# FNet mixing and a GELU block: column 128 of the second stage's operand gets products of its own

## The chip, the cores and the metric

The kernel runs on one core of a Trainium2 chip. The metric is the device time of one execution in microseconds (us). It was taken five times for the kernel before, and the median is compared. One execution more was recorded by the hardware profiler; all readings of the profile are from that one.

## The reference

Two blocks follow each other. The first takes, for each of 8 sequences of 3008 positions with 256 features, the real part of a Fourier transform over both axes. The second is a feed-forward block with weights of 256 x 2048 and 2048 x 256 and the quick form of GELU between them.

```python
X = np.fft.fft(x, axis=1)
X = np.fft.fft(X, axis=2)
out = X.real                      # (8, 3008, 256) float32
x2 = out.reshape(8 * 3008, 256)
h = x2 @ w_in                     # (24064, 2048)
g = h * (1.0 / (1.0 + np.exp(-1.702 * h)))
y = g @ w_out                     # (24064, 256)
```

## The kernel before

The transform over 3008 = 47 x 64 positions is done in two stages. The features are folded first: since the input is real, columns 0 to 128 of the folded operand carry the even part (the sums of feature d and feature 256 - d), columns 129 to 255 the odd part. The transform over the features itself is folded into the weights `wcs` of the feed-forward block.

The first stage (`mix1`, and `mix_first` for sequence 0) takes the products over the 47 positions of a residue class. Its results are written to DRAM (`spill`) and read back in another layout (`fill`) as the tile `t4`: 128 partitions, 12 groups (`NG`) and 256 columns. The partitions of `t4` are two halves of 64 rows (`u` = 0 and 1); in each half 32 rows hold the cosine and 32 the sine parts.

The second stage (`stage2(b, blk)`, line 337) makes from four groups of `t4` the two planes `pq[:, 0]` and `pq[:, 1]` of one block of sequence `b`. Three blocks (`NBLK`) make a sequence, and 24 blocks the run. Its weights are `m2` (`m2f` for sequence 0): 128 partitions, two sets of 64 columns, the cosine set (index 0) and the sine set (index 1), each used in two runs of 32 columns (`h`). Its 32 products run in four nested loops: `cs` over the two planes, `h` over the two runs, `g` over four slices of 32 columns, `u` over the two halves of the rows. Each product has 64 rows, 32 columns of weights and a moving operand of 4 groups by 32 columns; so it uses a 64 x 32 part of the array, and the eight products of one `cs` and `h` use eight different parts. The plane `cs` = 0 takes columns 0 to 127 of `t4` with the cosine weights, the plane `cs` = 1 takes columns 128 to 255 with the sine weights. Four transposes on VectorE (line 354) bring the result into `pq`.

Column 128 (the first one of the plane `cs` = 1) belongs to the even part, yet meets the sine weights there. So `rotate` (line 330) prepares it: one product over all 128 rows with the table `rot`, which exchanges the cosine and the sine rows with a sign, into a PSUM bank `psr`, and a copy back over column 128 of `t4`. It is called nine times: for groups 0 to 3 of sequence 0 just ahead of `stage2(0, 0)` with the copy on ScalarE, for groups 4 to 11 of sequence 0 at step 4, and once for each of the sequences 1 to 7, at step 36 of the sequence ahead (39 for the first), with the copies on VectorE. The stage for that sequence's block 0 is called at step 40.

The order of the work is written out by hand. The main loop has 384 steps, 48 for a sequence (3 blocks, 2 halves, 8 pairs of feed-forward columns). Each step issues the products of the feed-forward block (`halves`, line 495, and `small_products`, line 659), the activations and the sums, and at its end whatever `at(t, ...)` has registered for it: loads, folds, `mix1`, `rotate`, `spill`, `fill` and `stage2`. The engines run their queues in this order and wait for each other by semaphores.

The PSUM banks of the opening (before step 8) are handed out in a round robin of six (`spare`, line 164): each call of `bank` without a tag takes the bank that was handed out longest ago. `rotate` takes one for `psr` like everything else. At step 5 the list is made anew from the banks `o2`, `o3`, `o4` in their order at that time and `b2`; the products `pa` and `pb` of `hidden(5)` go to `b0` and `b1` by name. From step 8 on, `rotate` takes `b2`.

The table `small`, with `m2f`, `m2`, `rot` and the weights `cd` of the features, is loaded by one DMA on SyncE's queue between the first two parts of `w_in` (line 842).

Of the kernel before, what the change touches and what calls it, by code (L numbers as in the profile page):

```python
# [27 lines left out]
F32 = mybir.dt.float32  # L28
# [6 lines left out]
NA, NB = 47, 64  # L35
NJ = NB // 2
# [3 lines left out]
NU, NG = 2, 12  # L40
RUN = 32
# [9 lines left out]
def free(ap, offset, *dims):  # L51
    return bass.AP(ap.tensor, ap.offset + offset, [list(ap.ap[0])] + [list(d) for d in dims])


def kp(u, a):

    n, i = a // 4, 2 * (a % 4) + u
    return 8 * n + i if n else 7 - i


def tables(S, D):

    assert S == NA * NB and D == 256
    H = D // 2
    ks = np.array([kp(u, a) for a in range(NG) for u in range(NU)])
    s = NB * np.arange(NA)[:, None, None] + np.arange(NB)[None, :, None]
    angle = 2.0 * np.pi * ((s * ks) % S) / S
    cos, sin = np.cos(angle), np.sin(angle)
    w1 = np.zeros((NA, NJ + 3, NG * NU, 2))
    w1[:, 1:NJ, :, 0], w1[:, 1:NJ, :, 1] = cos[:, 1:NJ], sin[:, 1:NJ]  # L70
    e0, o0, e1, o1 = ENDS
    w1[:, e0, :, 0], w1[:, o0, :, 0], w1[:, e1, :, 1], w1[:, o1, :, 1] = cos[:, 0], sin[:, 0], cos[:, NJ], sin[:, NJ]


    w0 = np.zeros((128, NJ + 1, NG * NU, 2))
    low, high = w0[0:2 * NA:2], w0[1:2 * NA:2]
    low[:] = w1[:, :NJ + 1]
    high[:, 1:NJ, :, 0], high[:, 1:NJ, :, 1] = cos[:, NJ + 1:], -sin[:, NJ + 1:]
    high[:, e0, :, 1], high[:, o0, :, 1] = cos[:, NJ], sin[:, NJ]
    odd = np.arange(128)[:, None] % 2  # L80
    kinds = np.concatenate([1.0 - odd, odd, -1.0 * odd, 1.0 - 2.0 * odd], 1)

    c, q = np.divmod(np.arange(NJ), 16)
    m2 = []
    for jj in np.where(c, 16 + q, np.where(q, 16 - q, 0)), 4 * (q // 2) + 2 * (q % 2) + c:
        j, k2 = jj[:, None], np.arange(NB)[None, :]
        beta = 2.0 * np.pi * ((j * k2) % NB) / NB
        m = np.zeros((NU, 2, NJ, 2, NB))
        m[:, 0, :, 0], m[:, 1, :, 0] = np.cos(beta), -np.sin(beta)
        m[:, 0, :, 1], m[:, 1, :, 1] = np.sin(beta), np.cos(beta)  # L90
        m[:, :, 0, 0] = m[:, :, 0, 1] = np.stack([np.ones(NB), 1.0 - 2.0 * (np.arange(NB) % 2)])
        m2.append(m)
    rot = np.zeros((NU, 2, NJ, NU, 2, NJ))
    for i in range(NU):
        for n in range(NJ):
            rot[i, 0, n, i, 1, n], rot[i, 1, n, i, 0, n] = (1.0, -1.0) if n else (0.0, 0.0)
        rot[i, 0, 0, i, 0, 0] = rot[i, 1, 0, i, 1, 0] = 1.0

    m, d = np.arange(D)[:, None], np.arange(H)[None, :]
    phi = 2.0 * np.pi * ((m * d) % D) / D  # L100
    cd = np.stack([np.cos(phi), -np.sin(phi)], 1)
    cd[:, 1, 0] = 1.0 - 2.0 * (np.arange(D) % 2)
    cd = cd.reshape(2, H, 2, H).transpose(1, 0, 2, 3)
    small = [t.reshape(128, -1) for t in (*m2, rot, cd)]
    pad = 64 - NM
    w1 = np.pad(w1.reshape(NA, -1), ((0, 128 - NA), (0, pad)))
    w0 = np.concatenate([w0.reshape(128, -1), np.zeros((128, pad)), kinds], 1)
    return np.concatenate([w0, w1], 1).astype(np.float32), np.concatenate(small, 1).astype(np.float32)
# [3 lines left out]
def kernel(ctx: ExitStack, tc, x, w_in, w_out, tab1, tab2, out):  # L112
    nc = tc.nc
    B, S, D = x.shape
    DF = w_in.shape[1]
    H = D // 2
# [4 lines left out]
    const = ctx.enter_context(tc.tile_pool(name="const", bufs=1, space=SB))  # L121
# [10 lines left out]
    Td = [nc.dram_tensor(f"Td{b}", (NG * 128, D), F32, kind="Internal").ap() for b in range(B)]  # L132

    w1 = const.tile([128, (NJ + 3) * NM + 64 - NM], F32, tag="w1", name="w1")
    small = const.tile([128, 4 * NB + 128 + 4 * H], F32, tag="small", name="small")
    m2f, m2 = (small[:, i * 2 * NB:(i + 1) * 2 * NB].rearrange("p (c n) -> p c n", c=2) for i in range(2))
    rot = small[:, 4 * NB:4 * NB + 128]
    cd = small[:, 4 * NB + 128:].rearrange("p (i c d) -> p i c d", i=2, c=2)
    wcs = [const.tile([128, DF], F32, tag=f"wcs{i}", name=f"wcs{i}") for i in range(2)]

    wot = const.tile([128, 2, NF // 2, 4, H], F32, tag="wo", name="wo")
# [24 lines left out]
    def bank(name, tag=None):  # L166
        if tag is None:
            tag = spare.pop(0)
            spare.append(tag)
        if tag in ("o0", "o1"):  # L170
            return o_banks[int(tag[1])]
        return (rest if tag[0] == "o" else psp).tile([128, 512], F32, tag=tag, name=name)
# [5 lines left out]
    t4t, pqt, nbt = {}, {}, {}  # L178
# [148 lines left out]
            t4t[b] = tp.tile([128, NG, D], F32, tag="t4", name="t4")  # L327
        nc.sync.dma_start(out=t4t[b][:, a0:a1, :], in_=Td[b].rearrange("(a p) d -> p a d", p=128)[:, a0:a1, :])

    def rotate(b, a0=0, a1=NG, copy=None):  # L330

        col = t4t[b][:, a0:a1, H]
        ps = bank("psr")
        nc.tensor.matmul(ps[:, 0:a1 - a0], lhsT=rot, rhs=col, start=True, stop=True)
        (copy or nc.vector.tensor_copy)(col, ps[:, 0:a1 - a0])

    def stage2(b, blk):

        pq, t4 = pqp.tile([128, 2, 512], F32, tag="pq", name="pq"), t4t[b]
        pqt[b, blk] = pq  # L340
        m = m2 if b else m2f
        ps = [bank("ps2") for _ in range(NU)]
        for cs in range(2):
            for h in range(2):
                for g in range(4):
                    for u in range(NU):
                        rows, at = slice(64 * u, 64 * u + 64), cs * 256 + h * 128
                        nc.tensor.matmul(ps[u][32 * g:32 * g + 32, at:at + 128], lhsT=m[rows, cs, h * RUN:(h + 1) * RUN],  # L348
                                         rhs=t4[rows, 4 * blk:4 * blk + 4, cs * H + 32 * g:cs * H + 32 * g + 32],
                                         start=(cs == h == 0), stop=True, skip_group_check=True)  # L350
        for u in range(NU):
            for cs in range(2):

                nc.vector.transpose(free(pq[:], cs * 512 + u * RUN, [256, 2], [NU * RUN, 4], [1, RUN]),
                                    free(ps[u][:], cs * 256, [128, 2], [32, 4], [1, 32]))
# [32 lines left out]
    def squares(key, eng):  # L388
        g, hi = pre[key][0], raw[key][:, :, 1].bitcast(F32)
        if eng is nc.scalar:  # L390
            eng.activation(g[:], hi, ACTF.Square)
        else:
            eng.tensor_tensor(g[:], hi, hi, op=ALU.mult)

    def clamp(key, lo=0, n=1024):
        nc.gpsimd.tensor_scalar(pre[key][1][:, lo:lo + n], raw[key][:, lo:lo + n, 1].bitcast(F32), scalar1=TOP, scalar2=-TOP,
                                op0=ALU.min, op1=ALU.max)
# [490 lines left out]
    prepare(out0)  # L888
    finish_in(1)
    clamp(out0)  # L890
    rotate(0, 0, 4, nc.scalar.copy)
    squares(out0, nc.scalar)
    stage2(0, 0)
    warm(1)
    low_up(out0)
# [11 lines left out]
    def at(t, fn, *args):  # L907
        extra.setdefault(t, []).append((fn, args))

    n = len(steps)  # L910
# [11 lines left out]
    if B > 1:  # L922
        at(3, turn, 1)
        at(3, load_x, 1)
    at(4, rotate, 0, 4, NG)
    for i in range(NCK):
        at(7 + i, differences, i)
        at(8 + i, small_weights, i)
    for b in range(B):
        t0 = b * NBLK * NF  # L930
        late = 0 if b else 5
        if b + 2 < B:
            at(t0 + 10, turn, b + 2)
        if b + 1 < B:
            for c in range(NCH):
                for part in range(2):
                    at(t0 + 6 + 2 * c + part + late, fold1, b + 1, c, part, nc.gpsimd)
                if c % 2:
                    at(t0 + 9 + 2 * c + late, mix1, b + 1, c // 2)
            at(t0 + 24 + late, spill, b + 1)  # L940
            at(t0 + 29 + late, fill, b + 1)
            if b + 2 < B:
                at(t0 + 33 + late, load_x, b + 2)
            at(t0 + 36 + 3 * (late > 0), rotate, b + 1)
        for blk in range(NBLK):
            nxt = (b, blk + 1) if blk + 1 < NBLK else (b + 1, 0)
            if nxt[0] < B:
                at(t0 + blk * NF + 8, stage2, *nxt)
                at(t0 + blk * NF + 9, nyquist, *nxt)

    for t in range(n + LAG):
        if t < NP:
# [20 lines left out]
            if t == NP - 1:  # L973
                doubled(NP)
                middle(NP + 1)
        else:
            after, special = (any(fn in (mix1, stage2) for fn, _ in extra.get(k, ())) for k in (t - 1, t))
            if t < n:
                begin(t, 1)
# [78 lines left out]
```

## Time and profile before

| | |
|---|---|
| median of five runs | 1876.68 us |
| lowest and highest of them | 1874.21 and 1879.91 us |
| the profiled execution, its time | 1878.87 us |
| its span, from the first to the last instruction | 1876.8 us |
| mean granted TensorE clock | 0.998 |
| products of the second stage, L348 (records) | 1536 |
| transposes behind them, L354 | 96, mean 416 ns, 28.6 us of waiting for L348 in all |
| corrections, L334 (records) | 18 |
| their copies, L335 | 8 on VectorE, median 173 ns; 1 on ScalarE, 165 ns |

By stretches of the span, the busy time of the engines in us is:

| stretch | length | PE | DVE | ACT | POOL | DMA share |
|---|---|---|---|---|---|---|
| 0 to 37 | 37.0 | 32.0 | 26.9 | 21.7 | 17.0 | 0.85 |
| 37 to 60 | 23.0 | 22.2 | 20.2 | 19.3 | 13.1 | 0.99 |
| 60 to 90 | 30.0 | 29.6 | 19.4 | 18.0 | 14.7 | 0.71 |
| 90 to 125 | 35.0 | 32.0 | 31.2 | 15.7 | 27.6 | 0.47 |
| 125 to 350 | 225.0 | 221.3 | 185.0 | 135.8 | 121.5 | 0.32 |
| 350 to 1876.8 | 1526.8 | 1516.8 | 1249.0 | 938.7 | 770.2 | 0.31 |

PE is TensorE's matmuls, PEld its loads of weights, DVE VectorE, ACT ScalarE, POOL GpSimd, SP SyncE. A product in float32 leaves two loads and two matmul records (two passes), so a count of records is twice the count of products. [...] the pace is read from the distance of the starts. A line number in the profile is that of the kernel before.

### The profile page before, as it was taken

How to read it: one execution, taken by the hardware profiler on the slowest of the kernel's cores; microseconds unless marked ns; L12 is line 12 of the kernel's file. 1: busy time of each engine (PE TensorE's matmuls, PEld its weight loads, DVE VectorE, ACT ScalarE, POOL GpSimd, SP SyncE). 2: the span in 40 equal slices, each digit the busy share in tenths (PEclk: the TensorE clock that was granted, in tenths of full speed). 3: DMA queues.
4: the chain of work that ended last, by engine and by line, in shares of the span. 5: the costliest groups of instructions: out<-in, count | busy, mean ns of one | idle time of the engine just before them, and what ended most of it. 6: DMA issues, size and time to landing. Idle time of an engine off the chain costs nothing.

```text
span 1876.8 us, 55597 instructions
## 1 busy us (share of the span) xinstructions
PE 1853.8 (99%) x23600; PEld 1422.2 (76%) x23600; DVE 1531.7 (82%) x2245; ACT 1149.3 (61%) x2248; POOL 964.1 (51%) x1058
## 2 busy tenths in 40 slices
PE   8999999999999999999999999999999999999998
PEld 5567778777777777777777777777789777778776
DVE  7788878888889887988788877898788888878874
ACT  6655656666566665666565665656666666656663
POOL 4577335754467443674346733486334754444442
PEclk9999999999999999999999999999999999999999
DMA  8732351335312362304613165042631231212211
GB/s 276 179 51 17 80 84 24 51 51 112 30 16 48 51 124 19 51 13 83 93 16 52 23 113 57 13 63 44 110 28 24 19 51 47 27 17 18 20 22 23
DMA packets 145415, 105.21 MB, mean 56 GB/s; under 512 B 104914, under 2 KB 127986, under 8 KB 143984
## 3 DMA queue, kind: packets, MB, share of 16 engines
q1 hardware_dynamic: 143952, 101.14, 32.7%
q8 instruction: 186, 3.05, 0.7%
q10 hardware_dynamic: 1216, 0.52, 0.1%
q14 instruction: 61, 0.50, 0.1%
HBM read 58.38 MB, written 48.01 MB: 57 GB/s over the span
## 4 chain that ended last, share of the span: by engine, by line
PE 89%; DVE 5%; ACT 3%; DMA 1%; issue 1%; POOL 1%; SPq 0%; DVEq 0%; ACTq 0%; POOLq 0%
PE x L495 33%; PE o L495 25%; PE low L659 23%; PE o L659 4%; DVE big L625 2%; PE ps L348 1%; PE ps L246 1%; DVE big L762 1%; DVE big L539 1%; ACT x L566 1%; DMA big<-in_moe_w_in_dram 1%; PE psw L461 1%; ACT xt L249 1%; ACT big L581 0%; DVE big L671 0%
## 5 line engine op out<-in xcount | busy, mean ns | idle before, releaser
L596 POOL TENSOR_TENSOR big<-big 128x256 f32<-128x256 f32 (+1 forms) x376 | 349.8, 930 | 848.7 <-ACT big L588 733.5
L495 PE MATMUL x<-pq,wcs 128*64 128x256 f32 (+1 forms) x6016 | 778.8, 378 | 6.1 <-ACT x L566 3.0
L625 DVE TENSOR_TENSOR big<-big 128x512 f32<-128x512 f32 (+1 forms) x736 | 639.5, 883 | 30.9 <-PE low L659 14.5
L495 PE MATMUL o<-big,wo 128*64 128x256 f32 (+1 forms) x4800 | 627.8, 375 | 0.4 <-DVE big L603 0.4
L495 PEld LDWEIGHTS x<-pq,wcs 128*64 128x64 f32 x6016 | 419.9, 137 | 192.0 <-issue 14.9
L495 PEld LDWEIGHTS o<-big,wo 128*64 128x64 f32 x4800 | 348.2, 137 | 144.6 <-DVE big L603 1.2
L578 ACT ACTIVATE g<-x 128x512 f32<-128x512 f32 (+1 forms) x376 | 221.6, 589 | 376.8 <-PE x L495 375.7
L539 DVE TENSOR_TENSOR big<-g,x 128x512 f32<-128x512 f32 (+2 forms) x440 | 254.1, 589 | 204.3 <-ACT big L581 203.6
L659 PE MATMUL low<-big 128*64 128x128 f32 (+1 forms) x5888 | 386.8, 271 | 2.2 <-issue 2.2
L659 PEld LDWEIGHTS low<-big 128*64 128x64 f32 x5888 | 342.0, 137 | 29.9 <-issue 2.4
L566 ACT ACTIVATE x<-nb,af 128x256 f32<-128x256 f32 (+1 forms) x752 | 352.8, 469 | 12.2
L597 POOL TENSOR_TENSOR big<-big 128x256 f32<-128x256 f32 (+1 forms) x376 | 359.1, 955 | 0.0
L581 ACT ACTIVATE big<-x 128x512 f32<-128x512 f32 (+1 forms) x376 | 220.4, 586 | 202.5 <-PE x L495 189.8
L588 ACT ACTIVATE big<-big 128x512 f32<-128x512 f32 (+1 forms) x376 | 231.8, 616 | 44.7 <-DVE big L539 43.3
L659 PE MATMUL low<-big,wo 128*64 128x128 f32 (+1 forms) x2944 | 224.4, 271 | 0.1
L659 PEld LDWEIGHTS low<-big,wo 128*64 128x64 f32 x2944 | 176.0, 137 | 3.6 <-DVE big L625 0.4
L604 DVE TENSOR_TENSOR big<-big 128x512 f32<-128x512 f32 (+1 forms) x188 | 149.5, 795 | 6.5
L603 DVE TENSOR_TENSOR big<-big 128x512 f32<-128x512 f32 (+1 forms) x188 | 137.1, 729 | 4.7 <-POOL big L596 4.7
L659 PEld LDWEIGHTS o<-big,wo 128*64 128x64 f32 x1472 | 94.5, 138 | 24.2 <-issue 0.3
L762 DVE TENSOR_TENSOR big<-big,low 128x512 f32<-128x512 f32 (+3 forms) x184 | 109.0, 609 | 4.6 <-PE low L659 1.2
L659 PE MATMUL o<-big,wo 128*64 128x128 f32 (+1 forms) x1472 | 112.1, 271 | 0.0
L218 POOL TENSOR_TENSOR xt<-xt 111x510 f32<-111x510 f32 x56 | 76.7, 1370 | 4.4
(103 smaller groups left out, 976.4 us busy)
## 6 DMA issues: line engine op xcount, KB each, us to landing
out_dram<-os SPq DMA_DIRECT2D x284, 64.0 KB
Td<-xt SPq DMA_DIRECT2D x14, 768.0 KB
t<-Td SPq DMA_DIRECT2D x7, 1536.0 KB
xt<-in_x_dram SPq DMA_DIRECT2D x14, 512.0 KB
xt<-Xr SPq DMA_DIRECT2D x14, 512.0 KB
nb<-pq SPq DMA_DIRECT2D x23, 256.0 KB
out_dram<-os SPq DMA_DIRECT2D x96, 56.0 KB
Xr<-in_x_dram SPq DMA_DIRECT2D x7, 752.0 KB
```

The lines of the kernel that those rows point to most:

```text
L495: nc.tensor.matmul(out[c0:c0 + 64], lhsT=lhs[:, c0:c0 + 64], rhs=rhs, skip_group_check=True, **how)
L539: nc.vector.tensor_tensor(free(out, at + m - 1, [by, 2], [RUN, blocks], [-1, m]), *ins, op=op)
L566: nc.scalar.activation(x[:, i * 256:i * 256 + n], nbt[b, blk][:, hh * 256:hh * 256 + n], ACTF.Copy, scale=af1[:, f:f + 1])
L578: nc.scalar.activation(two(g[:], n), two(xb[t][:], n), ACTF.Copy, scale=2.0)
L581: nc.scalar.activation(front(t), two(xb[t][:], width(t)), ACTF.Gelu_apprx_sigmoid)
L588: nc.scalar.activation(back(t), back(t), ACTF.Gelu_apprx_sigmoid)
L596: eng.tensor_tensor(right(t, S1, n), left(t, A21, n), right(t, A22, n), op=ALU.add)
L597: eng.tensor_tensor(left(t, S3, n), left(t, A11, n), left(t, A21, n), op=ALU.subtract)
L603: eng.tensor_tensor(s2, s1, a11, op=ALU.subtract)
L604: eng.tensor_tensor(s4, a12, s2, op=ALU.subtract)
L625: nc.vector.tensor_tensor(out, i0, i1, op=how)
L659: nc.tensor.matmul(o, lhsT=lhs, rhs=rhs, start=first_in, stop=(p == NP - 2), skip_group_check=True)
```

## The change

Column 128 of `t4` keeps what `fill` brought. In the plane `cs` = 1, the product for the first slice (`g` = 0, columns 128 to 159) is split in two: one for column 128 alone with the cosine weights (4 moving columns, one of each group), one for columns 129 to 159 with the sine weights (124 moving columns). Both use the same part of the array and come one after the other, for `u` = 0 and then for `u` = 1. A block has 36 products instead of 32. The function `rotate`, its nine calls with their copies, and the table `rot` (128 of the 896 columns of `small`) are taken out.

```diff
-    rot = np.zeros((NU, 2, NJ, NU, 2, NJ))
-    for i in range(NU):
-        for n in range(NJ):
-            rot[i, 0, n, i, 1, n], rot[i, 1, n, i, 0, n] = (1.0, -1.0) if n else (0.0, 0.0)
-        rot[i, 0, 0, i, 0, 0] = rot[i, 1, 0, i, 1, 0] = 1.0
-
...
-    small = [t.reshape(128, -1) for t in (*m2, rot, cd)]
+    small = [t.reshape(128, -1) for t in (*m2, cd)]
...
-    small = const.tile([128, 4 * NB + 128 + 4 * H], F32, tag="small", name="small")
+    small = const.tile([128, 4 * NB + 4 * H], F32, tag="small", name="small")
...
-    def rotate(b, a0=0, a1=NG, copy=None):
-
-        col = t4t[b][:, a0:a1, H]
-        ps = bank("psr")
-        nc.tensor.matmul(ps[:, 0:a1 - a0], lhsT=rot, rhs=col, start=True, stop=True)
-        (copy or nc.vector.tensor_copy)(col, ps[:, 0:a1 - a0])
-
     def stage2(b, blk):
...
                         rows, at = slice(64 * u, 64 * u + 64), cs * 256 + h * 128
-                        nc.tensor.matmul(ps[u][32 * g:32 * g + 32, at:at + 128], lhsT=m[rows, cs, h * RUN:(h + 1) * RUN],
-                                         rhs=t4[rows, 4 * blk:4 * blk + 4, cs * H + 32 * g:cs * H + 32 * g + 32],
-                                         start=(cs == h == 0), stop=True, skip_group_check=True)
+                        o = ps[u][32 * g:32 * g + 32, at:at + 128].rearrange("p (a d) -> p a d", a=4)
+                        d0 = cs * H + 32 * g
+                        parts = ((0, 0, 1), (1, 1, 32)) if d0 == H else ((cs, 0, 32),)
+                        for c, lo, hi in parts:
+                            nc.tensor.matmul(o[:, :, lo:hi], lhsT=m[rows, c, h * RUN:(h + 1) * RUN],
+                                             rhs=t4[rows, 4 * blk:4 * blk + 4, d0 + lo:d0 + hi],
+                                             start=(cs == h == 0), stop=True, skip_group_check=True)
...
-    rotate(0, 0, 4, nc.scalar.copy)
...
-    at(4, rotate, 0, 4, NG)
...
-            at(t0 + 36 + 3 * (late > 0), rotate, b + 1)
```

More of the change, by code (lines that the diff above doesn't have):

```diff
@@ L134 @@
     w1 = const.tile([128, (NJ + 3) * NM + 64 - NM], F32, tag="w1", name="w1")
-    small = const.tile([128, 4 * NB + 128 + 4 * H], F32, tag="small", name="small")
+    small = const.tile([128, 4 * NB + 4 * H], F32, tag="small", name="small")
     m2f, m2 = (small[:, i * 2 * NB:(i + 1) * 2 * NB].rearrange("p (c n) -> p c n", c=2) for i in range(2))
-    rot = small[:, 4 * NB:4 * NB + 128]
-    cd = small[:, 4 * NB + 128:].rearrange("p (i c d) -> p i c d", i=2, c=2)
+    cd = small[:, 4 * NB:].rearrange("p (i c d) -> p i c d", i=2, c=2)
     wcs = [const.tile([128, DF], F32, tag=f"wcs{i}", name=f"wcs{i}") for i in range(2)]
```

## The prediction

> **What bounds the kernel now.** I read the page's busy shares first, then the chain of waits, then the two places that the change touches in the timeline of the PE, and last the single records there (every product leaves two weight loads and two matmul records, two passes).
>
> ```profile
> PE 1853.8 (99%) x23600; PEld 1422.2 (76%) x23600; DVE 1531.7 (82%) x2245; ACT 1149.3 (61%) x2248; POOL 964.1 (51%) x1058
> ...
> PE 89%; DVE 5%; ACT 3%; DMA 1%; issue 1%; POOL 1%; SPq 0%; DVEq 0%; ACTq 0%; POOLq 0%
> ```
>
> TensorE is the bound: 99% busy and 89% of the chain that ended last. A change of its work counts one for one; work on DVE or ACT counts only where PE waits for it. The chain around one correction (L334) and around the block of the second stage (L348) that follows it; the columns are start, length and what:
>
> ```profile
> 459.82 1.31 PE low L659 x24
> 461.13 0.32 PE psr L334 x2
> 461.45 1.01 PE x L495 x8
> ...
> 478.50 1.31 PE low L659 x24
> 479.81 1.09 PE ps L348 x64
> 480.89 1.01 PE x L495 x8
> ```
>
> Both lie on the chain with nothing but PE before and behind: no wait for the correction's copy or for the load of t4. Now the PE's timeline, first at a correction, then at a turn from L659 to L495 with none between:
>
> ```profile
> 460.09 1.04 PE L659 MATMUL low<-big 128*64 128x128 f32 x16
> 461.06 0.39 PE L334 MATMUL psr<-t,small 128*128 128x12 f32 x2
> 461.38 1.08 PE L495 MATMUL x<-pq,wcs 128*64 128x256 f32 x8
> ...
> 464.90 0.61 PE L659 MATMUL low<-big,wo 128*64 128x128 f32 x8
> 465.33 0.60 PE L495 MATMUL o<-big,wo 128*64 128x256 f32 x4
> ```
>
> The shape before the tile names is the part of the array used: 128*64 around, 128*128 in the correction. With it, 0.203 us pass from the last L659 start to L334, 0.133 between its two passes, 0.189 to L495 and 0.267 to the second pair of L495: 0.792 us. Without it the same two starts lie 0.102 + 0.216 = 0.318 apart. One correction costs 0.47 us, far more than its 12 columns, because the array changes its shape twice. That short products are limited by the load of their weights is read from the lines of L471 and L348 (least, median and longest duration in ns, first and last start):
>
> ```profile
> L471 PEld LDWEIGHTS psf<-twos,wcs x32: 181/187/187, 32.5 to 75.9; 1*128 1x128 f32 x32
> L471 PE MATMUL psf<-twos,wcs x32: 237/245/266, 32.5 to 75.9; 1*128 1x1 f32 x32
> ...
> L348 PEld LDWEIGHTS ps<-t,small x1536: 102/106/108, 33.8 to 1755.0; 64*32 64x32 f32 x192
> ```
>
> L471 streams one column, yet its passes start 0.1115 us apart: the time to load 128 columns of weights. A load for stage 2 has 32.
>
> [...] 0.20 us in front of L334 and of L348, and in the first mixing step the 129-column passes of one tile start at 342.381 and 342.491 while three others run 256 columns. [...] the trace has 24 ns of delay in the first passes of stage 2 (0.133 instead of 0.109). The trace has no short product in a small tile.
>
> **The change part by part.** The sum stands against the profiled execution, span 1876.8 us (1878.87 with what lies around it, 2.2 above the median of the runs); the difference is then put on the median, 1876.68.
>
> Removed: nine corrections. Seven (L334 from 244.7 to 1590.9 us) stand in the steady part: 7 x 0.474 = 3.3 us. The one at 33.5 is free: after the first block PE waits for POOL anyway,
>
> ```profile
> 36.51 1.55 PE L461 MATMUL psw<-wst,small 128*128 128x512 f32 x3 [0.49 <-POOL wst L437]
> ```
>
> The one at 63.95 costs 0.47, but without its bank the round robin shifts by one, and hidden(5) gets b1, which hidden(4) used as pa and which DVE L539 reads until 65.05. Its second half would start at about 64.7 and must wait for that: I take 0.1 of the 0.47 (bounds 0 and 0.5). The nine copies (0.17 us each on DVE, one on ACT) are worth nothing: DVE reaches the copy at 464.7, 3.3 us after its product at 461.4, and PE starts no stage behind it for 15 us. The table shrinks by 64 KB of 448; at the 262 GB/s of the first 37 us that is at most 0.25 us earlier for what follows in SP's queue; I take 0.1. Gains: 3.5 us (bounds 3.2 and 4.1).
>
> Added: in every block, for h = 0 and 1 and both row halves, one product more. 4 x 24 = 96 products, 192 loads and 192 passes of 4 columns; the full product loses 4 of 128 columns (3 ns a pass). Of the 24 blocks the first is hidden by the wait above; 23 count. What one block pays, called X, is worked out from the records of the block at 479.73. Eight tiles run side by side, each pass 0.109 us. Count the products from 0. In the half cs = 1 the load of product 17 starts at 480.169, 25 ns after product 1 has ended (second pass 479.875 + 0.269); that of product 25 at 480.388, 26 ns after product 9 ended (480.093 + 0.269). So only 16 products, 64 instructions, are under way, in order of the program, and new ones come in 17 ns apart. The last, 31, starts its second pass at 480.623; from there 0.199 to L495.
>
> With the change the half has 20 products. Products 18 and 19 are now the short and the long one of the same tile. 18 comes in at 480.186, [...] 19's first pass at 480.271, its second 0.105 later at 480.376; it ends at 480.645. Product 35, the last, may not come in before that: 480.67, or 480.69 behind 33 and 34 which wait for product 17 likewise. Its passes then start at about 480.72 and 480.82, against 480.623: X is 0.17 to 0.20. [...] If the window did not bind, only the four entries count: 4 x 17 = 0.07. If a short pass is no cheaper than a full one, 0.109, X is 0.38. I take 0.20: 23 x 0.20 = 4.6 us. Nothing covers it: behind the block PE goes on with L495. The four transposes (L354) wait 1.7 us for the block already, and the bank they free, the bias written into it and the next step's products shift with PE.
>
> Sum: 4.6 - 3.5 = +1.1 us.
>
> **The rivals.**
> A, as above: X between 0.17 and 0.23, +0.4 to +1.8 us. For it: the 16-product window explains the two odd delays of 81 ns in each block to 2 ns. About 1877.8.
> B, the short products are nearly hidden, X = 0.07: 1.6 - 3.5 = -1.9 us, 1874.8. For it: tiles are independent and the tile g = 0 is ahead, its last pass at 480.523 against 480.623. Against it: the records of products 17 and 25.
> C, the other side: a short pass in a 64*32 tile costs what a full one does, or products of one tile back to back hold up those behind. X = 0.38: 8.7 - 3.5 = +5.2, 1881.9. It decides from X = 0.32, where 23 X passes 3.5 + 3.75. For it: no such product is in the trace, and each pass is a load and a start more. Against: L471's starts are explained by its load.
> D, the opening pays more than I see: PE is idle for 9.2 us of the first 125 (37.0 - 32.0, 23.0 - 22.2, 30.0 - 29.6, 35.0 - 32.0 in the windows), and bank order and table size are changed there. If 5.1 us of that went, a little over half, the sum would be 1.1 - 5.1 = -4.0, 1872.7. Against: those waits are for POOL, DMA and ACT, which lose nothing of size.
> That the correction is not needed any more is exact: column 128 is real, so it takes the cosine weights; nothing else depends on the copy.
>
> **How the numbers follow.** Within 0.2% is +-3.75 us, about what a measurement of this kernel can tell from no change. A 0.46, all within; B 0.16, of which 0.04 falls below with a gain in the opening; C 0.26, of which 0.02 stays within; D 0.12, of which 0.02 stays within. Faster 0.04 + 0.10 = 0.14; within 0.46 + 0.12 + 0.02 + 0.02 = 0.62; slower 0.24. Predicted is A, 1877.8. A's own range, with 1.5 us for the scatter of a median (the runs span 1874.2 to 1879.9), is 1875.5 to 1880; reaching to B and C, 1873.5 to 1882.5.
>
> **What would show it.** L334 and L335 gone, and the turns there at 0.318 us. Blocks of L348 with 72 passes, from first to last start 0.89 us now, 1.09 expected; 0.96 is B, 1.27 is C. The starts of the short passes: 29 ns apart is my step, [...] 109 C. L348's last start to L495 still 0.20. In the opening, a wait of hidden(5) for L539. I am wrong if X lies outside 0.1 to 0.3, or if the steady part loses or gains with the blocks and turns as said.

## The result: 0.41% slower in the median, and a profile that doesn't show it

The changed kernel takes 1885.06 us in the median of 25 executions, the kernel before 1876.89 in that of 43. The ratio is 1.0041, with a 95% interval of 1.0031 to 1.0051: slower by 8 us, where 1 us was forecast. What stands out more than the median is the scatter. The executions of the kernel before span 1874.1 to 1881.4 us, those of the changed kernel 1875.5 to 1891.6.

The profiled execution of the changed kernel took 1876.92 us, 8 us below its median. Its page has this for the busy time and the chain that ended last:

```profile
span 1875.1 us, 55937 instructions
...
PE 1853.2 (99%) x23774; PEld 1416.3 (76%) x23774; DVE 1525.4 (81%) x2237; ACT 1149.8 (61%) x2247; POOL 963.0 (51%) x1058
...
PE 89%; DVE 5%; ACT 3%; DMA 2%; issue 1%; POOL 0%; SPq 0%; DVEq 0%; ACTq 0%; POOLq 0%
```

TensorE has 174 records more than before (192 of the short products, less 18 of the corrections), is as busy as before, and the span is 1.7 us shorter. The chain around the same block of the second stage as was shown of before, and PE's timeline there (L338 is the stage, L485 and L649 were L495 and L659):

```profile
477.10 1.31 PE low L649 x24
478.41 1.28 PE ps L338 x50
479.69 1.01 PE x L485 x8
```

```profile
477.69 0.72 PE L649 MATMUL low<-big 128*64 128x128 f32 x10
478.34 1.35 PE L338 MATMUL ps<-t,small 64*32 64x128 f32 x72
479.62 0.87 PE L485 MATMUL x<-pq,wcs 128*64 128x256 f32 x6
```

The reader is to see 72 records instead of 64 and 1.28 us on the chain instead of 1.09: a block costs 0.19 us more. From its first matmul start to its last it is 1.080 us, before 0.888; 22 of the other 23 blocks agree to 2 ns (the third waits for the first stage's evacuation).

So this profile agrees with the sum of the prediction, and says nothing of the 8 us. The place where it could come from is in both pages, and was passed over. PE's waits, longest first, of the kernel before and then of the changed one (columns: who waited for whom, total us, times, longest):

```profile
PE x L495 <- ACT x L566: 3.0, 5, 2.2
PE warm L317 <- DVE wcs L827: 2.6, 1, 2.6
PE psw L461 <- POOL wst L437: 2.6, 4, 1.4
PE x L495 <- ACT g L578: 2.4, 7, 0.4
PE low L659 <- issue: 2.2, 1, 2.2
PE ps L246 <- issue: 1.3, 1, 1.3
```

```profile
PE o L649 <- issue: 2.3, 1, 2.3
...
PE x L485 <- issue: 0.2, 1, 0.2
```

"issue" is idle time for which the profile shows no releaser: no semaphore that PE waited for ended it. The one of 2.2 us ends at 262.57 us in the kernel before, that of 2.3 us at 261.62 in the changed one. The page has a DMA queue of instructions, q8, with packets of 16 KB:

```profile
q8 instruction: 187, 3.06, 0.7%
```

Its packets go with the records of PE and PEld: 47695 of these and 186 packets before, 48047 and 187 now, 256 to 257 for each packet. So they are taken for PE's instructions, in blocks of 256, and the starts of the single packets show where PE had to wait for one. In the usual case the packet of a block starts when PE has passed some 180 records since a fixed multiple of 256. In front of the four stops of these two traces it starts at 419 to 445, which is 237 to 263 records or 8 to 9 us late, and PE stops 193 or 194 records past a multiple, which is taken for the end of a block. These four fall due just behind a block of the second stage or while `x` is loaded, when the DMA engines are full with data: the time that their packets took is 0.87 to 1.08 of the 16 engines' time in the four delays. This is theory F (fetch), formed on these two traces, and the runs were made to try it. (Some of the forecasts below say 10 us for the delay.)

### The profile page after: what moved, and what is told of

It is laid out like the page before. It is cut to its first block, busy times and chain, and to the rows that moved or that the text cites. A ratio compares the mean times of both kernels' runs of the same rounds, so it can differ in the third digit from the quotient of the medians.

```text
span 1875.1 us, 55937 instructions
## 1 busy us (share of the span) xinstructions
PE 1853.2 (99%) x23774; PEld 1416.3 (76%) x23774; DVE 1525.4 (81%) x2237; ACT 1149.8 (61%) x2247; POOL 963.0 (51%) x1058
## 4 chain that ended last, share of the span: by engine, by line
PE 89%; DVE 5%; ACT 3%; DMA 2%; issue 1%; POOL 0%; SPq 0%; DVEq 0%; ACTq 0%; POOLq 0%
PE x L485 33%; PE o L485 25%; PE low L649 24%; PE o L649 4%; PE ps L338 2%; DMA big<-in_moe_w_in_dram 1%; DVE big L615 1%; PE ps L239 1%; DVE big L752 1%; DVE big L529 1%; ACT x L556 1%; ACT xt L242 0%; ACT big L571 0%; DMA wo<-in_tab_dram 0%; DVE big L661 0%
## 5 line engine op out<-in xcount | busy, mean ns | idle before, releaser
L485 PE MATMUL x<-pq,wcs 128*64 128x256 f32 (+1 forms) x6016 | 773.0, 377 | 6.2 <-ACT x L556 3.0
L485 PE MATMUL o<-big,wo 128*64 128x256 f32 (+1 forms) x4800 | 622.9, 375 | 0.4 <-DVE big L593 0.4
L485 PEld LDWEIGHTS x<-pq,wcs 128*64 128x64 f32 x6016 | 412.9, 137 | 195.8 <-ACT x L556 15.7
L485 PEld LDWEIGHTS o<-big,wo 128*64 128x64 f32 x4800 | 343.5, 137 | 146.2 <-DVE big L593 1.2
L529 DVE TENSOR_TENSOR big<-g,x 128x512 f32<-128x512 f32 (+2 forms) x440 | 254.1, 589 | 206.8 <-ACT big L571 205.9
L649 PE MATMUL low<-big 128*64 128x128 f32 (+1 forms) x5888 | 382.8, 271 | 0.0
L649 PEld LDWEIGHTS low<-big 128*64 128x64 f32 x5888 | 338.2, 137 | 28.3
L649 PE MATMUL low<-big,wo 128*64 128x128 f32 (+1 forms) x2944 | 221.2, 271 | 0.1
L649 PEld LDWEIGHTS low<-big,wo 128*64 128x64 f32 x2944 | 172.8, 137 | 3.6 <-DVE big L615 0.4
L649 PEld LDWEIGHTS o<-big,wo 128*64 128x64 f32 x1472 | 93.2, 138 | 27.4 <-issue 2.7
L649 PE MATMUL o<-big,wo 128*64 128x128 f32 (+1 forms) x1472 | 111.2, 271 | 2.3 <-issue 2.3
```

The lines of the kernel that those rows point to most:

```text
L485: nc.tensor.matmul(out[c0:c0 + 64], lhsT=lhs[:, c0:c0 + 64], rhs=rhs, skip_group_check=True, **how)
L529: nc.vector.tensor_tensor(free(out, at + m - 1, [by, 2], [RUN, blocks], [-1, m]), *ins, op=op)
L649: nc.tensor.matmul(o, lhsT=lhs, rhs=rhs, start=first_in, stop=(p == NP - 2), skip_group_check=True)
```

## The experiments

Each version was timed beside the kernel before on the same chip; ratios are against it, with their 95% intervals. The profiled execution of a version is one of its executions.

**The change again, and its two parts alone.** First the changed kernel once more, then the split without the removal, the removal without the split (it leaves column 128 uncorrected), and the change with the opening of before. In this excerpt of the edits, the first pair of lines turns the products of the change into those of the split alone, the next three lines are what the removal alone takes out of the kernel before, and the last two stand in the fourth version:

```diff
-                        parts = ((0, 0, 1), (1, 1, 32)) if d0 == H else ((cs, 0, 32),)
+                        parts = ((1, 0, 1), (1, 1, 32)) if d0 == H else ((cs, 0, 32),)
...
-    rotate(0, 0, 4, nc.scalar.copy)
-    at(4, rotate, 0, 4, NG)
-            at(t0 + 36 + 3 * (late > 0), rotate, b + 1)
...
+    bank("psr")
+    at(4, bank, "psr")
```

> The changed kernel unaltered, to see a second profile of it and the scatter of its single executions. Its profiled execution agrees with the sum of the prediction (span 1875.1 us, each block of stage 2 longer by 0.19 us), but its 25 executions spread from 1875.5 to 1891.6 us, where the kernel before spreads from 1874.1 to 1881.4. Theory F (fetch): TensorE runs out of instructions while a chunk of them is being fetched behind data transfers; a profile of a long execution shows several idle stretches of PE of about 2 us with no releaser, at a few places, and blocks of unchanged length. Theory S (short products): the blocks themselves vary; a long execution shows blocks of stage 2 well over 1.08 us. Expected by F: median near 1884, spread 10 us or more, and if the profile falls on a long execution, 2 to 7 idle stretches of 2 us.

> The kernel before with the first slice of the plane cs = 1 split into 4 and 124 columns, both with the sine weights; the corrections stay. By the sums of the prediction: 23 x 0.19 = +4.4 us over the kernel before, about 1881, with the scatter of before. By theory F the scatter depends on how many instructions TensorE has per sequence (here 48 more than before, where the change has 44 more or so), so it should widen as with the change: 1880 to 1895, median over +8. By theory O (the opening, its bank order or the smaller table is the cause) the scatter is that of the kernel before, 7 us.

> The kernel before without its nine corrections and otherwise unchanged, so column 128 stays uncorrected; the table keeps its size, the opening's bank order is that of the change. By the sums: -3.4 us, about 1873.5. Theory F: TensorE has about 4 instructions less per sequence, a small shift, so little change of scatter. Theory O (bank order): wide scatter, up to 15 us, as with the change.

> The change with the table of its old size and a bank taken (and left unused) where the corrections of sequence 0 took theirs, so memory layout and the opening's bank order are those of before; the products of stage 2 are those of the change. Theory O: back to the scatter of before, median about 1878. Theory F and theory S: as the change, median 1883 to 1886 and a spread of 10 us or more.

| version | median us | lowest and highest | ratio | span of its profile | PE stops without releaser in it |
|---|---|---|---|---|---|
| change again | 1885.56 | 1878.35 to 1891.51 | 1.0047 (1.0030 to 1.0063) | 1876.6 | 3.1 |
| split alone | 1895.23 | 1891.45 to 1903.52 | 1.0106 (1.0085 to 1.0127) | 1901.5 | 15.0 |
| removal alone | 1879.48 | 1874.80 to 1886.01 | 1.0017 (1.0009 to 1.0024) | 1878.4 | 7.0 |
| change, old opening | 1883.73 | 1878.73 to 1889.53 | 1.0035 (1.0020 to 1.0050) | 1877.7 | 2.8 |

The parts don't add up. The split alone costs 19 us where its blocks explain 4.4; the removal, which only takes work away, costs 3 us, and its scatter of 11 us is wider than theory F had forecast. The opening is not the cause: with the table and the banks of before the change is still 1.0035. The split's profile is its longest execution and shows what happens in one. Its waits of PE, then the chain and the timeline around one of the stops, and the DMA issues of SyncE's queue ahead of it (L499 and L663 are the former L495 and L659, L352 the second stage, L803 the stores, L322 the spill, L366 the broadcast of the row `nb`):

```profile
PE low L663 <- issue: 7.2, 2, 3.8
PE x L499 <- issue: 6.5, 3, 3.9
...
PE ps L246 <- issue: 1.3, 1, 1.3
```

```profile
1095.92 0.66 PE ps L352 x21
1096.58 1.01 PE x L499 x8
1097.59 1.29 PE o L499 x12
1098.89 0.44 PE low L663 x8
1099.32 0.93 PE x L499 x8
1100.25 0.21 PE low L663 x3
1100.46 3.36 issue
1103.83 1.65 PE low L663 x13
```

```profile
1100.08 0.38 PE L663 MATMUL low<-big 128*64 128x128 f32 x3
1103.83 0.80 PE L663 MATMUL low<-big 128*64 128x128 f32 x5 [3.36 <-issue]
```

```profile
1082.64 6.74 SPq L803 DMA_DIRECT2D out_dram<-os  x12
1091.54 0.79 SPq L322 DMA_DIRECT2D Td<-xt  x2
1098.07 0.54 SPq L366 DMA_DIRECT2D nb<-pq  x1
```

PE breaks off in the middle of a run of products of one kind, with no semaphore to release it, for 3.36 us. In the packets of q8, one started at 1083.28 and the next only at 1101.63, 265 records later than usual; PE goes on 2.2 us after that. Taken at its usual place it would have started at about 1093.9. From there to 1101.6 the DMA engines moved the 96 packets of 16 KB of the spill and began on the 128 of 2 KB of the broadcast, which take about 1.08 us each. The same happens at 645.09 and 1561.44 us, in every other sequence, at the same place behind a block. The blocks themselves keep their length (1.078 to 1.080 us, the third apart), so theory S falls. A stop has an aftermath. The stretch before, the stop, and the 3.4 us behind it:

```profile
0.00:1099.60 1099.60, 1076.92 (x13638) 824.42 (x13640) 897.65 (x1308) 667.82 (x1297) 589.35 (x651) 1.00 0.37 67
1099.60:1103.90 4.30, 0.94 (x12) 0.50 (x9) 0.56 (x1) 1.96 (x4) 1.40 (x2) 0.91 0.85 52
1103.90:1107.30 3.40, 3.40 (x27) 3.06 (x28) 0.69 (x1) 0.27 (x1) 0.00 (x0) 0.61 0.82 27
```

The third number from the end is the granted clock of TensorE: 0.61 in the 3.4 us behind the stop. The records have it at half speed behind each of the five stops of over 1 us in this trace, four times for 3413 ns and once for 6827. An estimate of what a stretch of 3413 ns adds is half of it, 1.7 us.

**The place in the chunks, and the broadcast.** If stops depend on where the fetches fall, more PE instructions in the opening for the same columns of array time must move the median. And if the broadcast makes fetches late, half of it at a time must help. The broadcast went in two parts of 64 partitions, two steps apart, in both kernels; in the kernel before, the six warm-up products of 512 columns became 24 of 128 or 48 of 64:

```diff
-            nc.sync.dma_start(out=nb[:], in_=free(row, 0, [0, 128], [1, 512]))
+            nc.sync.dma_start(out=nb[64 * part:64 * part + 64], in_=free(row, 0, [0, 64], [1, 512]))
...
+                at(t0 + blk * NF + 11, nyquist, *nxt, 1)
...
-    warm(6)
+    ps = bank("warm")
+    for _ in range(24):
+        nc.tensor.matmul(ps[0:128, 0:128], lhsT=wcs[0][:, 0:128], rhs=wcs[0][:, 0:128], start=True, stop=True)
```

> The change, with the broadcast of the row nb (L352) in two transfers of 64 partitions, two steps apart, instead of one of 128. In the traces so far a fetch of 256 instructions for TensorE that falls due just behind a block of stage 2 starts up to 10 us late while that broadcast (128 packets of 2 KB, 1.08 us each) and what is queued with it fills the DMA engines, and TensorE stops when the fetch starts some 10 us late. Theory F: with half of it at a time the delay behind a block falls to about 5 us and the stops behind blocks go; median about 1877 to 1879, spread 5 us or less. Theory S or any cause in the products of stage 2: no change, median 1885, spread over 10 us.

> The kernel before with the same two halves of the broadcast. Theory F: it loses its few stops behind blocks, median 1874 to 1876, and b1 lies 1 to 2 us above it, which is the sum of the prediction. Rival R (the change costs about 8 us by itself, wherever the broadcast stands): b1 lies 7 to 9 us above it.

> The kernel before with its six warm-up products of 512 columns in the opening replaced by 24 of 128 columns: the same columns of array time, 72 instructions of TensorE more, all of them in the first 10 us. Nothing behind it changes but the place of every later instruction in the chunks of 256 that are fetched. Theory F: the median moves by some us, either way (the stops depend on where the fetches fall), and the scatter with it. Theory S and rival R: 1876, as before.

> As b3, with 48 products of 64 columns and 64 weights: 168 instructions of TensorE more in the first 10 us. Theory F: again another median and scatter, and not the same as b3. Theory S and rival R: 1876, as before.

The change with halves stayed at 1884.59 (1.0031, 1.0019 to 1.0044), spread 14 us: a miss for the expectation that the broadcast alone was to blame. The kernel before with halves came to 1875.72, 0.9984 (0.9977 to 0.9991), with its 17 executions between 1872.2 and 1877.4. So the two lie 8.9 us apart, as rival R had said and not theory F. The pads gave 1883.58 (1.0023, 1.0012 to 1.0033) and 1882.68 (1.0026, 1.0016 to 1.0035): more time from the same work. But not all of this is stops. In their profiles the third block of the second stage starts 2.8 and 2.2 us later than in the kernel before, at 176.23 and 175.61 against 173.46, so a good half came in the opening (2.0 us of it in one wait for DVE near 117 us, which occurs in other versions too). Beside that there are stops at new places, the longest at 642.8 and 800.2 us in the one, 411 and 569.6 in the other, where the kernel before has none. The pads support theory F for the places, less for the size.

**Catching a long execution, and moving the spill.** The change profiled twice more, the change with the spill two steps and the fill one step later, and the change with the pad of 72:

```diff
-            at(t0 + 24 + late, spill, b + 1)
-            at(t0 + 29 + late, fill, b + 1)
+            at(t0 + 26 + late, spill, b + 1)
+            at(t0 + 30 + late, fill, b + 1)
```

> The changed kernel unaltered, one look, to catch a long execution in a profile (the two profiles of it so far fell at 1876.9 and 1878.4 us, below its median of 1885). Theory F: if the look falls at 1884 us or more, its trace has PE stops of 2 us and more with no releaser near 634, 1084 or 1536 us, where a fetch starts late behind the block of stage 2, the stores and the spill (the fetches of the short executions there start 7 to 9 us late, just not late enough). Theory S: blocks of stage 2 longer than 1.08 us.

> The change with the spill two steps later (26 instead of 24) and the fill one step later (30 instead of 29), so that the spill no longer stands in SyncE's queue right behind the stores and the block of stage 2 of the same step. Theory F in its second form (the stops of the long executions come from the fetches at 626, 1077 and 1529 us, held up by stores, spill and broadcast together): median 1877 to 1880 and the spread halves. If the stops fall elsewhere: no gain, median 1883 or more.

> The change with the six warm-up products of the opening as 24 of 128 columns, 72 instructions of TensorE more in the first 10 us. Theory F: every later fetch falls due some 3 us earlier against the transfers, so median and spread move, either way, by 3 us or more. Otherwise: 1885 with the spread of the change.

> As the first run of this set: the change unaltered, one look more for a long execution.

These profiles fell at 1877.92 and 1875.91 us: all four of the change lie at the low end of its scatter, and its long executions are in no trace. With the later spill: 1881.85, 1.0023 (1.0013 to 1.0032), its 10 executions between 1878.8 and 1884.7. More than half of the spread was gone, but only 4 us of the 8, short of what was expected. With the pad: 1884.20, 1.0036 (1.0023 to 1.0048), the median the same, the spread 4 us instead of 16, in 5 executions. Its profile, at 1884.5, shows stops in four lines of its waits:

```profile
PE ps L239 <- issue: 3.0, 2, 1.8
PE low L649 <- issue: 2.8, 1, 2.8
...
PE o L485 <- issue: 0.9, 1, 0.9
...
PE x L485 <- issue: 0.4, 1, 0.4
```

They lie at 260.4, 414.8, 867.7, 1024.7 and 1478.1 us; but for the first, none of these is in the four profiles of the change. The pad moved the stops to other fetches. The forecast had the median move by 3 us or more; it did not. If theory F holds, that the two medians agree is chance, and no run tried this.

**Both crowds thinned, in both kernels.** By theory F a fetch is late behind all that stands before it, so thinning one crowd may leave the other. The row `nb` went through DRAM instead of from one partition to all: in the traces its 128 packets then take 0.08 us each in most cases instead of 1.08. This alone, and with the later spill as well:

```diff
+            if part == 0:
+                nc.sync.dma_start(out=view(Nd, at_, [512, 1], [1, 512]), in_=row)
+            else:
+                nc.sync.dma_start(out=nb[:], in_=view(Nd, at_, [0, 128], [1, 512]))
...
+                at(t0 + blk * NF + 10, nyquist, *nxt, 1)
```

> The change, with the row nb first written to DRAM (2 KB) and one step later read from there to 128 partitions, instead of 128 packets from one partition at 1.08 us each. Theory F: the fetches behind a block of stage 2 are no longer late by up to 10 us (delay under 5 us in the trace), and the median falls by some us, to 1877 to 1881. If the broadcast has no part in the long executions of the change: 1884 to 1886.

> The kernel before with the same way through DRAM. Theory F: 1873 to 1876, as with the two halves (which gave 0.9984 of before), and d1 above it by less than the 8 us of the pair before and after.

> d1 with the spill two steps and the fill one step later as well, so that both crowds behind a block of stage 2 (broadcast; stores and spill) are thinned. Theory F: the best of the versions of the change, 1874 to 1878, spread 5 us or less. Rival R (the change costs some 8 us by itself): 1883 or more.

> The kernel before with both edits of d3. Theory F: 1872 to 1876, and d3 lies 0 to 3 us above it: what is left is the sum of the prediction, +1.1 us. Rival R: d3 lies 7 us or more above it.

| | before's products and corrections | the change |
|---|---|---|
| as they were | 1877.21 us, 1874.3 to 1881.0 | 1.0041 (1.0031 to 1.0051) |
| `nb` through DRAM | 1874.08, 0.9986 (0.9980 to 0.9992) | 1884.73, 1.0039 (1.0027 to 1.0052) |
| and the spill later | 1874.60, 0.9986 (0.9980 to 0.9993) | 1876.79, 1.0002 (0.9994 to 1.0010) |

The ratio in the first row is that of the result, from another chip; the other numbers are of one chip. The way through DRAM alone missed its forecast: it took 3 us off the kernel before and nothing off the change, and the two lie 10.7 us apart. In the profile of d1 the fetch at 635.83 us, behind the spill, is still 219 records late. In the last row the 13 executions of the change lie between 1876.0 and 1879.2 us; the spread of 16 us is gone, and the gap between the kernels fell from 8 to 2.2 us. Neither edit touches the second stage's products. Rival R, that the change costs 8 us by itself wherever the transfers stand, falls. It takes both edits: with the later spill alone the change kept 4 us, with the way through DRAM alone all of the 8. (The kernel before was not run with the later spill alone.) In the profile of d3 only one stop is left, the one near 262 us that every version has:

```profile
PE o L655 <- issue: 2.8, 1, 2.8
```

Apart from it, no packet of q8 in that trace starts more than 188 records late; in the profile of the change the one at 632.69, behind the spill, starts 215 late and that at 1394.51 237 late. The second is the stop of 0.2 us; so in these profiles the change has next to no margin at two places that d3 has cleared. Both d2 and d4 are faster than both kernels.

**The two terms of the sum alone, with the crowds thinned.**

> d4 (the kernel before with nb through DRAM and the later spill) without the nine corrections, so column 128 stays uncorrected. With the crowds thinned, the terms of the sum should be seen by themselves: -3.4 us against d4, so 1871 (1870 to 1873). In the kernel before itself the same edit (a3) gave +0.17% instead. If it lies at d4 or above, late fetches still take the gain, or the corrections cost nothing.

> d4 with the first slice of the plane cs = 1 split, both parts with the sine weights, corrections kept: +4.4 us against d4, so 1879 (1878 to 1881). In the kernel before itself the same edit (a2) gave +1.06%, 20 us. If it lies 10 us or more above d4, late fetches outlast the thinning in this place, or the split costs more than its blocks show.

Removal alone: 1872.19, 0.9959 (0.9946 to 0.9973) of before. Split alone: 1881.34, 1.0015 (1.0009 to 1.0022). Against d4's 0.9986 this is -0.27% and +0.29%, -5 and +5.4 us, with d4's own interval of +-1.2 us and theirs on top. The profiles are sharper, if the opening is left out, which by itself differs by up to 1.9 us between these four. The table has the stretch from the first start of the fourth block of the second stage to that of the last block; it holds 20 blocks and 6 corrections. From its length go PE's stops without releaser and what the half-speed stretches of the clock cost (half of their length, leaving out the part that lies in a stop). The last column is 0.192 us for each block and -0.474 for each correction:

| profile | length us | stops | half speed | rest | against its base | by the sum |
|---|---|---|---|---|---|---|
| before | 1504.2 | 3.5 | 1.7 | 1499.0 | | |
| the change | 1502.3 | 2.5 | 0 | 1499.8 | +0.8 | +1.0 |
| split alone (a2) | 1526.6 | 14.9 | 9.4 | 1502.3 | +3.3 | +3.8 |
| removal alone (a3) | 1505.9 | 6.9 | 3.4 | 1495.6 | -3.4 | -2.8 |
| d4, crowds thinned | 1499.6 | 1.4 | 0 | 1498.2 | | |
| the change (d3) | 1501.7 | 2.8 | 0 | 1498.9 | +0.7 | +1.0 |
| removal (e1) | 1497.1 | 1.9 | 0 | 1495.2 | -3.0 | -2.8 |
| split (e2) | 1506.3 | 2.3 | 1.7 | 1502.2 | +4.1 | +3.8 |

The reader is to see that the rest follows the sum to 0.6 us in every version, while stops and clock go their own way: of the 22 us that the split's stretch is longer than that of before, 19 are stops and half-speed clock. The parts do what was worked out, and what breaks the sum is beside them.

## Why the prediction was wrong

Its direction was right, +1.1 us in the forecast, but the size was not, and rival C, which ended on the slow side, gave a wrong reason for it. Most of the 8 us came from a side that the sum doesn't have, so the direction is luck.

- *A block of the second stage, X.* Taken as 0.20 us out of 0.17 to 0.20; measured 0.192. The working held: in the block at 478.34 the passes of a short product start 28 ns apart (478.801 and 478.829), where the prediction had 29; three of the block's four short products do so, and in the fourth it is 51 ns. From the trace of before the step is an estimate: L471's passes, with loads of 128 columns, start 0.1115 us apart, which makes 28 ns for the 32 columns here, and three such steps make 84 of the 85 ns from 480.186 to 480.271 in the prediction. The 0.23 at the upper end of A stood for slower starts, an assumption of the author's that no trace had shown; the three speak against it. The loads of the last two products start at 479.268 and 479.284, where the window of 16 products had put the last at 0.94 to 0.96 us behind the block's start (0.944 measured). Rivals B and C fall.
- *The corrections.* Seven times 0.474 us: the turn from L649 to L485 near 460 us takes 0.318 us in the changed trace, as forecast. Right.
- *The opening.* `hidden(5)` waits for the reader of its new bank, as was said: PE waits for DVE L529 once more than before, 0.3 us. Rival D falls: with the old opening (a4) the change is as slow.
- *The sum.* As the time of the array's work it holds: +0.8 us in the steady stretch of the change's own pair of profiles where the sum has +1.0. That their whole spans differ by -1.7 is luck of the pair: the kernel before has 1.0 us more of stops and one half-speed stretch (1.7 us) more. The spans of d3 and d4 differ by 0.4 us, their medians by 2.2.
- *The step that failed* is the first: "A change of its work counts one for one". It takes TensorE to be held up by nothing but its operands and its own pace. The text looked past lines of the profile that say otherwise, 3.5 us of "issue" in PE's waits, and put the effect on these at nothing without a reason: it priced the added instructions (352 records more in all, some 44 for each sequence) only by the time they take in the array, never by where they push every later one in the blocks of 256 in which they are fetched. The array's work cost what the sum says, about 1 us; the median moved by 8.2. The other 7 us are beside the array's work: with two edits of transfers alone the gap fell to 2.2 us.
- *What the text could have seen.* The margin: in the trace of before, the fetch at 1018.72 us started 246 records late and PE stopped for 1.3 us.

Shown is this. TensorE stops behind late fetches: the 20 profiles have 46 stops without releaser, and each lies 193 to 195 records past a multiple of 256, taken for the end of a block, behind a fetch that started 194 to 270 records late. 95 fetches of these profiles start over 200 records late, and in none of these delays do the DMA engines stand idle for more than 0.3 us. Edits of transfers alone close most of the gap (d3 against d4). The array's work of the change is worth what the sum says (e1, e2 and the table).

Not shown is a trace of a long execution of the changed kernel itself. That its other 7 us are stops for instructions follows from the edits that take them away and from the traces of a2, a3 and c3; it is not read from a record. The same edits also free the way for data, so it is not excluded that PE waits for late data in the long executions. One sign is on record for all of them, the granted clock: in the eight shortest of the 25 executions (mean 1878.7 us) it is 0.9979 in the mean, in the eight longest (1890.1 us) 0.9965. That is some 2.6 us of clock, and it fits stops: in the 20 profiles, past the opening and before the last 10 us, every half-speed stretch begins within 1.6 us of the end of a stop. How the fetches of the two kernels fall differently in a long execution is open too: in the profiles the latest fetches of both are alike (four latest 229 to 249 records before, 215 to 263 with the change). And the profiled executions of a4, b1, c2 and d1 lie at the low end of their scatter like the four of the change, which is hardly chance; why was not found.

## What to carry to other kernels

Instructions added to TensorE had two prices here: their own time, 0.192 us a block, and stops and half-speed clock, 19 of the 22 us that the split's stretch is longer than that of before. By theory F the second comes from the shift of all later instructions against the data transfers that their fetch must pass. When removing work makes a kernel slower, or a median moves by more than its profile explains, look for idle time without releaser, and hold the starts of the instruction queue's packets against the large transfers of the moment. Take the stops and the half-speed stretches out of a profile before two of them are compared. Compare the scatter of many executions and not one profile; and if a change of order makes the scatter small, measure the change again on top of that.

## What was not expected of the hardware

- TensorE stopped for 1.7 to 3.9 us, 22 times in the profiles, where the packet of its next 256 instructions started 235 to 270 records, 6 to 10 us, later than usual. Where PE had run dry before the packet started, it had passed up to 449 records since the multiple, against some 180 at the usual start of a packet.
- A packet of instructions started late while data moved: the one due at about 1093.9 us in the split's profile started at 1101.63, and in between the DMA engines moved 96 packets of 16 KB and began 38 of 2 KB.
- 128 packets of 2 KB from one partition took 1.08 us each in the kernel before; read from DRAM, most took 0.08.
- Of the 18 stops of 2 to 4 us in all profiles, 13 had TensorE's clock at half speed for 3413 ns or more, from within 1.4 us of their end.
- In a 64 x 32 tile the passes of a product of 4 columns start 28 ns apart, those of one of 128 columns 109, and only 16 products are under way at once (in the block at 479.73 of the kernel before, the loads of products 17 and 25 start 25 and 26 ns after products 1 and 9 have ended).
